# A planner with new step durations, a table of rank offsets, and a first layer that starts unit by unit

## The chip, the cores and the metric

The kernel runs on one core of a Trainium2 chip. The metric is the device time of one execution in microseconds (us), the median of several runs. TensorE (PE) does the matrix products, VectorE (DVE), ScalarE (ACT) and GpSimd (POOL) the elementwise work, and SyncE (SP) issues the transfers.

## The reference

Causal attention over 576 positions with 8 heads and 2 batches, mixed with a linear memory read-out, then two feed-forward layers in sequence:

```python
scores = scale * q @ k.T; scores[causal] = -1e9
local = softmax(scores) @ v
mem_out = (phi(q) @ M_prev) / (phi(q) @ z_prev + 1e-6)
x = g * mem_out + (1 - g) * local            # 1152 x 512
h = x @ w_in; x = elu(h) @ w_out             # 512 -> 2048 -> 512
p = probs / probs.sum(-1)
out = sum_e p[:, e] * (relu(x @ w1[e]) @ w2[e])   # 4 experts, 512 -> 1024 -> 512
```

## The kernel before

Each fp32 product is made of three products of rounded parts (`mm3`, L276: high x high, high x low, low x high). For each matrix the high part is an ACT copy to the rounded type, and the low part, here called the remainder, a subtraction on POOL (`part_l`, L247) or DVE. `w_in` and `w_out` come as 64-bit floats: each half tile of such a weight is loaded, then `upper` on ACT, `shift` and `lower` on DVE make an fp32 half of it (L211 to L238), which is also kept in DRAM for the second use.

The tokens are cut in two. Units F0 to F3 (two heads each) do attention for the first 384 tokens; units R00 to R13 for the other 768. A unit's steps (`plan_unit`, L1186) are named in the code: load, split_h/split_l (high part and remainder of queries and keys), phi (the memory features), mem, score, lowest, exp, trans, evac, values, sum, both, turn (a transposition), join (writes the input of the first layer). F3 is the "hurried" unit. While the R units run, the first 384 tokens go through the first layer (a0: four parts, each four "up" groups `ua` and four "down" groups `da`) and the experts (b0: `ub`, `db`). Then the R tokens go through both layers in a faster form with half sums (`Wide`; `plan_halves`; `x1.plan` makes the sums T1 to T4 of its input).

The order of instructions on each engine is written out by a planner (`Plan`, L1040). Every step has an engine, a cost in us, a rank, predecessors, and slots (buffers, PSUM banks) that it takes and gives. `order` runs a clock: an engine that is free takes the ready step with the lowest rank. For most slots the steps take them in the order in which they were added, whatever their rank; the banks "m" (three), "s0" and "s1" are exempt. The engines then run that order; semaphores make them wait for what they really need. A unit's rank is its start plus an offset per step (`OFFSET`, L163); R units start at 48 plus `STARTS2`, and none of their steps may start earlier than its rank less 4 (`EARLY`). A weight's rank is in `W_RANKS` (12, 26, 32, 38, 44) or follows the clock of the layer.

Where the plan sees PE wait over 0.3 us in the first 140 us, `keep_busy` puts products on a tile of zeros ahead of the step (L304), and at least one ahead of most PE steps of F units (`FEWEST`). `WARM` such products stand at the start.

A first-layer group takes one "m" bank and multiplies four chunks of 128 input rows (kk 0 to 3), which come from units F0 to F3 in this order. `group` (L344) puts it into the plan as two steps, kk 0 to 2 and kk 3; `before_up` (L358) makes both wait for all four units' joins. In F units the second score piece takes two "m" banks, a second transposition group and the turn one each.

## Time and profile before

| | us |
|---|---|
| median of 3 runs (718.53 to 719.46) | 719.34 |
| profiled execution | 718.8 |
| its span, first to last instruction | 717.0 |
| PE busy | 706.3 (99%) |
| POOL busy | 426.0 (59%) |
| DVE busy | 392.6 (55%) |
| ACT busy | 354.3 (49%) |

A PE that is shown as busy may run products on zeros; they have the line L304. "Releaser" names what ended a wait. In a table of windows each row is a stretch of the span: its length, the busy time of each engine with the number of its instructions, the granted TensorE clock, the share of the 16 DMA engines, and the rate.

### The profile page before, as it was taken

The page shows a single profiled execution, that of the slowest core. Times are in us where ns is not written, and L with a number is a line of the kernel's source. Part 1 is how long each engine was busy: PE and PEld are TensorE (multiplying, and loading weights), DVE is VectorE, ACT ScalarE, POOL GpSimd, SP SyncE. Part 2 cuts the span into 40 slices and gives each one's busy share as a digit, 9 for nine tenths or more (in the row PEclk, how much of TensorE's full clock was granted, in tenths as well). Part 3 has the DMA queues.
Part 4 walks back from the last instruction along what each step waited for, and adds up shares of the span by engine and source line. Part 5 has one row for each costly group of instructions (what it writes and reads, how often), then busy time and mean ns, then how long its engine had stood idle before and what let it go on. Part 6 is the DMA issues. An engine that isn't in the chain of part 4 may idle for free.

```text
span 717.0 us, 10716 instructions
## 1 busy us (share of the span) xinstructions
PE 706.3 (99%) x4099; PEld 640.0 (89%) x4099; DVE 392.6 (55%) x846; ACT 354.3 (49%) x610; POOL 426.0 (59%) x256
## 2 busy tenths in 40 slices
PE   9989999999999999998999999999999999999997
PEld 5769998988889889897999999998998989889896
DVE  3787785534453353454718466873645636354462
ACT  7868877453544443444867355752423423233120
POOL 5467886855546534179988564597646566564210
PEclk9999999999999999999999999999999999999999
DMA  8678983525133142031432111222211203121002
GB/s 288 231 266 319 370 324 118 195 95 172 53 127 118 49 129 88 31 118 59 133 118 89 59 59 59 62 80 66 88 60 59 92 26 118 35 83 59 1 1 88
DMA packets 23539, 82.21 MB, mean 115 GB/s; under 512 B 2880, under 2 KB 2880, under 8 KB 23488
## 3 DMA queue, kind: packets, MB, share of 16 engines
q1 hardware_dynamic: 23488, 81.53, 33.4%
q8 instruction: 32, 0.52, 0.3%
q14 instruction: 19, 0.16, 0.1%
HBM read 70.77 MB, written 10.75 MB: 114 GB/s over the span
## 4 chain that ended last, share of the span: by engine, by line
PE 88%; POOL 3%; DVE 3%; DMA 2%; ACT 2%; issue 1%; SPq 0%; DVEq 0%; ACTq 0%
PE db L278 9%; PE db L280 8%; PE db L279 8%; PE ov L1377 4%; PE da L278 4%; PE da L279 4%; PE da L280 4%; PE ub L278 3%; PE sR L1299 3%; PE tR L1361 3%; PE ub L280 3%; PE ub L279 3%; PE ov L1384 1%; PE om L1248 1%; PE ua L278 1%; PE ua L280 1%
## 5 line engine op out<-in xcount | busy, mean ns | idle before, releaser
L249 POOL TENSOR_TENSOR wl<-wr,wh 128x1024 fp32r<-128x1024 f32 x72 | 172.1, 2395 | 160.3 <-ACT wh L245 155.4
L245 ACT ACTIVATE wh<-wr 128x1024 fp32r<-128x1024 f32 x72 | 75.7, 1056 | 109.3 <-PE db L279 65.6
L278 PE MATMUL db<-wh,hb 128*128 128x512 f32 x288 | 115.0, 399 | 0.0
L280 PE MATMUL db<-wl,hb 128*128 128x512 f32 x288 | 112.7, 391 | 2.0 <-POOL wl L249 2.0
L279 PE MATMUL db<-wh,hb 128*128 128x512 f32 x288 | 112.3, 390 | 0.0
L997 DVE SCALAR_TENSOR_TENSOR acc<-db,pr,acc 128x512 f32<-128x512 f32 x42 | 31.5, 751 | 69.9 <-PE db L280 69.2
L280 PEld LDWEIGHTS db<-wl,hb 128*128 128x128 f32 x288 | 54.0, 188 | 13.9 <-POOL wl L249 2.4
L278 PE MATMUL da<-ha,wh 128*128 128x384 f32 x192 | 65.3, 340 | 0.0
L280 PE MATMUL da<-ha,wh 128*128 128x384 f32 x192 | 64.2, 335 | 0.0
L278 PEld LDWEIGHTS db<-wh,hb 128*128 128x128 f32 x288 | 54.2, 188 | 11.3 <-issue 1.4
L279 PE MATMUL da<-ha,wl 128*128 128x384 f32 x192 | 64.2, 334 | 0.0
L279 PEld LDWEIGHTS db<-wh,hb 128*128 128x128 f32 x288 | 54.2, 188 | 10.0
L278 PE MATMUL ub<-yh,wh 128*128 128x384 f32 x128 | 45.7, 357 | 0.0
L280 PE MATMUL ub<-yl,wh 128*128 128x384 f32 x128 | 43.0, 336 | 0.0
L279 PE MATMUL ub<-yh,wl 128*128 128x384 f32 x128 | 42.9, 335 | 0.0
L1377 PE MATMUL ov<-rvR,pfR 128*128 128x65 f32 x288 | 38.3, 265 | 0.0
L1377 PEld LDWEIGHTS ov<-rvR,pfR 128*128 128x128 f32 x288 | 37.2, 191 | 0.2
L278 PEld LDWEIGHTS da<-ha,wh 128*128 128x128 f32 x192 | 36.1, 188 | 0.5 <-issue 0.4
L279 PEld LDWEIGHTS da<-ha,wl 128*128 128x128 f32 x192 | 36.1, 188 | 0.0
L280 PEld LDWEIGHTS da<-ha,wh 128*128 128x128 f32 x192 | 36.0, 188 | 0.0
L1322 ACT ACTIVATE ptR<-ptR,nmR 128x576 f32<-128x576 f32 (+2 forms) x48 | 29.8, 659 | 10.3 <-DVE nmR L1313 10.2
L506 ACT ACTIVATE hb<-ub 128x384 fp32r<-128x384 f32 x32 | 15.7, 491 | 38.2 <-PE ub L280 38.2
(862 smaller groups left out, 1835.3 us busy)
## 6 DMA issues: line engine op xcount, KB each, us to landing
wr<-in_w SPq DMA_DIRECT2D x64, 512.0 KB, 3.7
w<-in_w SPq DMA_DIRECT2D x32, 512.0 KB, 6.5
wscr<-wr SPq DMA_DIRECT2D x16, 512.0 KB, 7.3
wr<-wscr SPq DMA_DIRECT2D x16, 512.0 KB, 3.3
rvR<-in_vm_r SPq DMA_DIRECT2D x8, 520.0 KB, 4.6
qkR<-in_qk_r SPq DMA_DIRECT2D x8, 480.0 KB, 4.9
rvF<-in_vm_f SPq DMA_DIRECT2D x4, 520.0 KB, 5.0
out<-acc SPq DMA_DIRECT2D x8, 256.0 KB, 2.0
```

Of the source, the lines that this page charges most:

```text
L245: nc.scalar.activation(out=t["wh"], in_=t["wr"], func=AF.Copy)
L249: nc.gpsimd.tensor_tensor(out=wl, in0=t["wr"], in1=f32(t["wh"]), op=ALU.subtract)
L278: nc.tensor.matmul(out, ah, bh, start=first, stop=False)
L279: nc.tensor.matmul(out, al, bh, start=False, stop=False)
L280: nc.tensor.matmul(out, ah, bl, start=False, stop=last)
L506: nc.scalar.activation(out=t["h"][:, 0], in_=t["ps"], func=AF.Relu)
L997: nc.vector.scalar_tensor_tensor(out=acc, in0=t["ps"], scalar=p, in1=acc, op0=ALU.mult, op1=ALU.add)
L1248: nc.tensor.matmul(pair("om", t, r0, r), unit["phi"][:, q:q + r], apart(MEMORY[kind] + 2 * bi), start=True, stop=True,)
L1299: nc.tensor.matmul(unit["s", odd, t, n][:, :w], unit[x][rows, q], unit[y][rows, ks[odd]], start=m == 0 and r0 == 0, stop=m == 2 and final,)
L1322: nc.scalar.activation(out=blk, in_=blk, func=AF.Exp, scale=-1.0, bias=unit["nm"][odd][:, k:k + 1])
L1361: nc.tensor.transpose(pst[:, P * n:P * n + P], src, ident)
L1377: nc.tensor.matmul(unit["ov"][:, odd, t], pf[:, col:col + P], unit["rv"][:, at_], start=False, stop=odd == 1 and j == nb - 1)
```

## The change

- The planner's cost functions and lags get other constants (`act_cost`, `dve_cost`, `values_cost`, `LAG`, some PE and DVE steps), and the least products on zeros are counted in PE steps.
- `Plan.alone`: steps in this set start only when POOL is free in the plan, and book POOL for their length. In it: `shift` and `lower` of the first three weights, the subtractions of the x sums, and `probs`.
- `MOVES`: offsets that `Plan.add` adds to the ranks, by unit, by step, by weight, by group.
- `before_up` of a0, part 0: kk 0 and 1 wait for F0 and F1, kk 2 for F2, kk 3 for F3; groups with fc over 1 wait for F3's turn besides. `group` takes a list of stages.
- F3's turn takes bank "t" in place of "m".
- F0's load is two transfers: keys first (`load_k`), then queries; its splits are three pieces, keys, the first 256 columns of queries, the rest. The first two scores wait for the first two pieces.
- `WARM` is 11 in place of 16; the plan's PE starts at `AWAKE`.

The diff, cut to its core:

```diff
+MOVES = {
+    ("F", "evac"): 6.5, ("F", "join_l"): -12, ("F", "load"): 3.5, ("F", "load_v"): -3, ("F", "phi_r"): 9,
+    ("F", "values"): -12, ("F0", "exp21"): 7, ("F0", "load_v"): 8, ("F0", "turn"): 14.5, ("F1", "exp21"): 13,
+    ("F1", "load"): 4, ("F2", "join_h"): 3.5, ("F2", "mem"): 5, ("F3", "score00"): 6.5, ("R", "exp"): -21.5,
+    ("R", "load_v"): -9, ("R", "mem"): -0.5, ("R", "phi_r"): -2.5, ("R", "score"): -17.5, ("R", "split_l"): 8.5,
+    ("R", "trans"): -10, ("R", "values"): -5.5, ("a0", "then", "d"): 8, ("a0", "then", "u", 1): -10.5,
...
+    ("v", "S2"): 14, ("v", 52): 4.5, ("w", "lower"): -11.5, ("w", "part_h"): 7, ("w", "part_l"): 16.5,
+    ("w", "shift"): 3.5, ("w", "upper"): -1.5, ("w", 0): 21, ("w", 1): 7.5, ("w", 14): 11.5, ("w", 2): -22.5,
+    ("w", 20): 18.5, ("w", 6): 14.5, ("w", 8): 4.5, ("w", 9): -20.5, "F0": 5, "F2": 9, "F3": 8, "R00": -28.5,
+    "R01": -28, "R02": -37.5, "R03": -9, "R10": -43.5, "R11": -6.5, "R12": -12.5,
+}
...
+        plan.alone.add(("probs",))
...
-    WARM = 16
+    WARM = 11
+    AWAKE = 2.66 + 0.218 * WARM
...
+                if i < W_EARLY:
+                    plan.alone |= {("w", i, f"{x}{half}") for x in ("shift", "lower")}
...
-            self.plan.add((*key, 0), "pe", 3 * cost, self.due, lambda: fn((0, 1, 2)), after, takes)
-            self.plan.add(key, "pe", cost, self.due, lambda: fn((3,)), [(*key, 0), *late], (), gives)
+            before, start = [], 0
+            for n, (upto, needs) in enumerate(stages):
+                name, last = (*key, f"k{n}"), upto == 4
+                self.plan.add(
+                    key if last else name, "pe", (upto - start) * cost + 0.04 * (n == 0), self.due,
+                    lambda kks=tuple(range(start, upto)): fn(kks), [*before, *needs], [] if n else takes, gives if last else (),
+                )
+                before, start = [name], upto
...
-            return [(f"F{c}", "join_l") for c in range(H // 2)], []
+            done = [[(f"F{c}", "join_l")] for c in range(H // 2)]
+            return [(2, done[0] + done[1] + [("F3", "turn")] * (fc > 1)), (3, done[2]), (4, done[3])]
...
+                    plan.alone.add((self.what, name, kk))
...
-        return 0.833e-3 * n + (0.09 if psum else 0.13)
+        return 0.833e-3 * n + (0.055 if psum else 0.095)
...
-        return 1.042e-3 * n + 0.115
+        return 1.042e-3 * n + 0.065
...
-        LAG = {"sync": 2.8, "pe": 0.2, "act": 0.13, "dve": 0.13, "pool": 0.1}
+        LAG = {"sync": 2.8, "pe": 0.2, "act": 0.16, "dve": 0.17, "pool": 0.12}
...
+            rank += sum(MOVES.get(x, 0.0) for x in families(key, engine))
...
+                        if key in self.alone:
+                            if free["pool"] > now + 1e-6:
+                                continue
+                            free["pool"] = now + cost
...
+        whole, keys, early = slice(0, nq + nk), slice(nq, nq + nk), slice(0, 2 * P)
+        if uid == "F0":
+            add("load_k", "sync", 0.8, lambda: load(keys), takes=["raw"])
+            add("load", "sync", 0.8, lambda: load(slice(0, nq)))
+            splits = [("0", keys, ["load_k"]), ("1", early, ["load"]), ("", slice(2 * P, nq), ["load"])]
...
-        x_from = "m" if spare else "t"
+        x_from = "m" if spare and not hurried else "t"
```

`families` gives the names under which a step looks up `MOVES`; all that match are added:

```python
def families(key, engine):
    name = str(key[0])
    if name[0] == "F":
        return [name, ("F", key[1].rstrip("0123456789")), key]
    if name[0] == "R":
        return [name, ("R", key[1].rstrip("0123456789"))]
    if name in ("w", "v"):
        return [(name, key[1]), (name, key[2].rstrip("0123456789") if name == "w" else key[2])]
...
```

## Rows read from the trace of the kernel before

**Rows 1.** Windows over the whole span: busy us of each engine, clock, DMA.
```profile
6.40:35.00 28.60, 28.07 (x248) 21.39 (x248) 19.03 (x83) 23.96 (x54) 15.75 (x11) 1.00 0.78 277
35.00:40.30 5.30, 4.31 (x29) 2.50 (x28) 4.45 (x9) 2.29 (x4) 1.70 (x1) 1.00 0.83 308
48.80:53.90 5.10, 3.50 (x22) 1.82 (x20) 4.82 (x10) 5.10 (x11) 5.10 (x5) 1.00 0.94 350
53.90:112.00 58.10, 57.81 (x366) 54.71 (x364) 48.49 (x97) 45.16 (x79) 44.13 (x28) 1.00 0.87 322
112.00:330.00 218.00, 218.00 (x1381) 194.01 (x1381) 98.76 (x252) 108.15 (x174) 122.26 (x69) 1.00 0.32 104
330.00:346.00 16.00, 13.58 (x66) 11.46 (x65) 5.03 (x9) 5.99 (x11) 15.53 (x10) 1.00 0.43 134
346.00:713.00 367.00, 367.00 (x1937) 343.99 (x1937) 203.81 (x377) 154.88 (x269) 213.57 (x120) 1.00 0.20 66
```

**Rows 2.** The same windows for the tile zeros alone (PE, PEld, DVE).
```profile
35.00:40.30 5.30, 2.56 (x12) 1.05 (x12) 0.00 (x0) 1.00 0.83 308
48.80:53.90 5.10, 2.38 (x12) 1.08 (x12) 0.00 (x0) 1.00 0.94 350
53.90:112.00 58.10, 1.27 (x7) 0.41 (x5) 0.00 (x0) 1.00 0.87 322
```

**Rows 3.** Waits of PE (total, times, longest), and the chain at 330 us.
```profile
PE db L280 <- POOL wl L249: 2.0, 1, 2.0
328.91 2.00 POOL xT4l L705 x2
330.91 2.31 POOL wl L249
```

**Rows 4.** Chain of waits from 35 to 59 us: start, us, what.
```profile
50.07 0.70 DVE wr L235
50.81 1.67 PE sR L304 x7
53.26 0.92 PE da L304 x5
54.18 0.17 PE da L278
```

**Rows 5.** Timeline: remainders of weights 0, 2 and 4, first uses of 0 and 4.
```profile
29.00 2.36 POOL L249 TENSOR_TENSOR wl<-wr,wh 128x1024 fp32r<-128x1024 f32 x1 [2.78 <-ACT wh L245]
40.27 0.47 PE L278 MATMUL ua<-xh,wh 128*128 128x384 f32 x1
44.68 2.42 POOL L249 TENSOR_TENSOR wl<-wr,wh 128x1024 fp32r<-128x1024 f32 x1 [3.71 <-ACT wh L245]
55.48 2.40 POOL L249 TENSOR_TENSOR wl<-wr,wh 128x1024 fp32r<-128x1024 f32 x1
58.35 0.44 PE L278 MATMUL ua<-xh,wh 128*128 128x384 f32 x1
```

**Rows 6.** The in-place shift (ns min/median/max), its longest, and POOL beside it.
```profile
L231 DVE TENSOR_SCALAR wr<-wr x6: 415/418/2180, 23.6 to 42.4; 128x512 int32<-128x512 int32 x6
38.60 2.36 POOL L249 TENSOR_TENSOR wl<-wr,wh 128x1024 fp32r<-128x1024 f32 x1 [5.72 <-ACT wh L245]
39.07 2.18 DVE L231 TENSOR_SCALAR wr<-wr 128x512 int32<-128x512 int32 x1
```

**Rows 7.** Timeline of the start, and the window with the highest DMA rate.
```profile
0.72 0.39 SPq L1164 DMA_DIRECT2D qkF<-in_qk_f  x1
4.06 0.99 ACT L1173 ACTIVATE qhF<-qkF 128x448 fp32r<-128x448 f32 x2 [2.07 <-DMA qkF<-in_qk_f]
6.41 0.36 PE L1299 MATMUL sF<-qhF 64*128 64x192 f32 x2
80.00:90.00 10.00, 10.00 (x60) 9.56 (x60) 8.39 (x17) 8.81 (x16) 8.75 (x6) 1.00 1.02 415
```

**Rows 8.** Chain of waits over the first 14 us.
```profile
2.10 6.55 DMA qkF<-in_qk_f
```

More of the change, by code (lines that the diff above doesn't have):

```diff
@@ L52 @@
 ]
+MOVES = {
[11 rows of a table added]
+}
[7 more added lines that the diff above has]
+        return [(name, key[1]), (name, key[2].rstrip("0123456789") if name == "w" else key[2])]
+    if name[0] in "ab":
+        return [(name, *key[1:3])] if engine == "pe" else [(name, "then", key[1]), (name, "then", key[1], key[-1])]
+    return [name, (name, key[1])] if name in "xy" else [name]
 def f32(ap):
@@ L342, in key, with group @@
             return (self.name, *a)
-        def group(self, key, cols, after, late, takes, gives, fn):
+        def group(self, key, cols, stages, takes, gives, fn):
             cost = 3 * (cols / 2400 + 0.0132)
@@ L382, in up @@
                 last = nb == len(self.blocks) - 1
-                early, late = self.before_up(part, fc)
+                first, *rest = self.before_up(part, fc)
                 self.group(
-                    key, n, [self.weights(part, fc // 2), *early], late,
+                    key, n, [(first[0], [self.weights(part, fc // 2), *first[1]]), *rest],
                     ["m"] + ["h"] * (nb == 0), ["w"] * (last and fc % 2), products,
@@ L544, in down @@
                 self.group(
-                    key, 512, [self.weights(part, 2), self.weights(part, 3), self.last_up(part)]
-                    + self.units(part, 0, 1, 2),
-                    self.units(part, 3), ["m"], (["w"] * 2 + ["h"] * 4) * last, products,
+                    key, 512,
+                    [(3, [self.weights(part, 2), self.weights(part, 3), self.last_up(part)] + self.units(part, 0, 1, 2)),
+                     (4, self.units(part, 3))], ["m"], (["w"] * 2 + ["h"] * 4) * last, products,
                 )
@@ L1047, in __init__ @@
             self.awake, self.last = 0.0, 0.0
+            self.alone = set()
         def add(self, key, engine, cost, rank, fn, after=(), takes=(), gives=(), slack=0.0, early=1e9):
+            rank += sum(MOVES.get(x, 0.0) for x in families(key, engine))
             self.steps[key] = (engine, cost, rank, fn, after, takes, list(gives), slack)
             self.first[key] = rank - early
-        def as_added(self):
-            for step in self.steps.values():
-                step[3]()
         def order(self, free=None):
@@ L1159, in add, with load @@
             )
-        def load():
-            unit["k"] = atile([P, NQ + KEYS["R"]], F32, tag="raw", name=f"qk{uid}")[:, :nq + nk]
-            nc.sync.dma_start(out=unit["k"], in_=qk[kind][c] if kind == "F" else qk[kind][b, c])
+        def load(cs):
+            if "k" not in unit:
+                unit["k"] = atile([P, NQ + KEYS["R"]], F32, tag="raw", name=f"qk{uid}")[:, :nq + nk]
+            nc.sync.dma_start(out=unit["k"][:, cs], in_=(qk[kind][c] if kind == "F" else qk[kind][b, c])[:, cs])
         def load_v():
@@ L1170, in split_h @@
         def split_h(cs):
-            if cs.start == 0:
+            if "h" not in unit:
                 unit["h"] = atile([P, NQ + KEYS["R"]], F32R, tag="qh", name=f"qh{uid}")[:, :nq + nk]
@@ L1175, in split_l @@
         def split_l(cs):
-            if cs.start == 0:
+            if "l" not in unit:
                 unit["l"] = atile([P, NQ + KEYS["R"]], F32R, tag="ql", name=f"ql{uid}")[:, :nq + nk]
@@ L1197, in phi @@
             nc.gpsimd.tensor_tensor(out=unit["phi"], in0=unit["e"], in1=unit["phi"], op=ALU.add)
-        add("load", "sync", 1.6, load, takes=["raw"])
+        whole, keys, early = slice(0, nq + nk), slice(nq, nq + nk), slice(0, 2 * P)
[3 more added lines that the diff above has]
+            splits = [("0", keys, ["load_k"]), ("1", early, ["load"]), ("", slice(2 * P, nq), ["load"])]
+        else:
+            add("load", "sync", 1.6, lambda: load(whole), takes=["raw"])
+            splits = [("", whole, ["load"])]
         add("load_v", "sync", 1.3, load_v, takes=["rv"])
-        pieces = [("0", slice(0, nq)), ("", slice(nq, nq + nk))] if uid == "F0" else [("", slice(0, nq + nk))]
-        for name, cs in pieces:
-            n, first = cs.stop - cs.start, cs.start == 0
-            add("split_h" + name, "act", act_cost(n), lambda cs=cs: split_h(cs), ["load"], ["qh"] * first)
+        for name, cs, loaded in splits:
+            n, first = cs.stop - cs.start, name == splits[0][0]
+            add("split_h" + name, "act", act_cost(n), lambda cs=cs: split_h(cs), loaded, ["qh"] * first)
             eng = ("dve", dve_cost(n)) if uid == "F0" else ("pool", pool_cost(n))
@@ L1210, in plan_unit @@
         if kind == "F":
-            add("phi_p", "act", act_cost(nq), phi_p, ["phi_e", "split_l"], gives=["raw"])
+            add("phi_p", "act", act_cost(nq), phi_p, ["phi_e", *(f"split_l{x}" for x, _, _ in splits)], gives=["raw"])
             add("phi", "pool", pool_cost(nq), phi, ["phi_p"], gives=["pe"])
@@ L1330, in plan_unit @@
                 f"score{t}{n}", "pe", score_cost(t, z_ - a), lambda t=t, n=n: score(t, n),
-                ["split_l"] + ["score{}{}".format(*pieces[0])] * (not first), s_from[t, n] + ["pt", "nm", "nm"] * first, ["qh", "ql"] * last,
+                [f"split_l{x}" for x, _, _ in splits[:2 if t < 2 else 3]] + ["score{}{}".format(*pieces[0])] * (not first), s_from[t, n] + ["pt", "nm", "nm"] * first, ["qh", "ql"] * last,
             )
@@ L1335, in plan_unit @@
                 add(
[L1336 removed]
+                    f"lowest{t}{n}{odd}", "dve", dve_cost(z_ - a) + 0.015,
                     lambda odd=odd, t=t, n=n: lowest(odd, t, n),
@@ L1441, in plan_unit @@
         add("turn", "pe", 0.11 * nt, turn, ["both"], [x_from], ["tv"])
-        done = [("m", (uid, "turn")) if spare else "t"]
+        done = [("m", (uid, "turn")) if x_from == "m" else "t"]
         if group:
@@ L1472, in tile_kernel @@
         plan, clock = Plan(SLOTS), [START2]
-        plan.awake, plan.last = IDLE_END, 0.43 * WARM - 0.5
+        plan.awake, plan.last = IDLE_END, AWAKE
         plan_small(plan, OFFSET["load"] + 3.0, 1.5)
@@ L1485, in tile_kernel @@
         x1.plan(plan, START2 + STARTS2[-1] + 8.0, lambda name, kk: [(f"R{b}{c}", "join_l") for b, c in units])
-        free = plan.order({"pe": 0.43 * WARM - 0.5})
+        free = plan.order({"pe": AWAKE})
     ps_g = ctx.enter_context(tc.tile_pool(name="ps_g", bufs=8, space=PSUM, reuse_waits="tile"))
```

32 lines of the change are left out of this document (16 added, 16 removed), and 2 rows, old and new, of the table MOVES.

## The prediction

> **What bounds the kernel now.** I read the stretches first. From 346 us to 713 us TensorE (PE) is busy all of the time, and so it is from 112 to 330 us; in these two stretches it runs real products back to back, so nothing that the planner reorders there can shorten them [rows 1]. That leaves 0 to 112 us and 330 to 346 us. A busy PE hides something there: the products on "zeros", which only keep the engine awake, count as work. The same windows for that tile alone show where [rows 2]. In 35.0 to 40.3 us PE is busy 4.31 us, 2.56 of it on zeros, so it works about 1.75 of 5.3 us and 3.6 us are lost. In 48.8 to 53.9 us it is 3.50 less 2.38, or 1.1 of 5.1 us, and 4.0 us are lost. In 53.9 to 112 us 1.3 us of zeros and 0.3 us of idle time are lost, 1.6 in all; in 330 to 346 us 2.4 us, of which 2.0 us is one wait for a weight remainder from GpSimd (POOL) [rows 3]. The zeros of 6.4 to 35 us I leave out: the kernel puts at least one ahead of most attention steps of the early units in either version. With 1.0 us at the start (below) the list is 1.0 + 3.6 + 4.0 + 1.6 + 2.4 = 12.6 us. That is what an order without any stall could win.
>
> **First layer unit by unit.** Before, every group of the first layer waits in the plan until all four early units F0 to F3 are joined. After, its first two input chunks wait for F0 and F1 only, the third for F2, the fourth for F3. The groups of fc 0 and 1 may open early, fc 2 and 3 only behind F3's turn. The opened groups can thus run three chunks of three products each ahead of F3's end: 2 x 9 = 18 products at 0.17 us [rows 4], or 3.1 us of real work into the 3.6 us that are lost now between 35.0 and 40.3 us. Weight 0, which both groups read, is ready at 29.00 + 2.36 = 31.4 us, 8.9 us ahead of its first use at 40.27 [rows 5], so there is room. The price is banks: an open group holds one of three "m" banks, and a second score piece of an F unit takes two of them at once. So the second group can only open once F3 has had that piece. F3's turn gets the bank "t" instead of "m", so that it can't wait for the groups that wait for it. Bounds: 0 (groups open only when F3 is done) and 3.1 us; I take 2.3, nearer to the upper, because most of the lost time lies behind F3's scores.
>
> **Ranks, durations, and the stall at 49 to 54 us.** The durations and ranks run nowhere; they change the order alone. The last row ahead of the stall is the conversion of a weight in the score banks: DVE's wr step at 50.07 us ends, then PE goes on with seven zeros, R00's scores, five zeros and the first down group [rows 4]. PE had nothing else: the R units may not start before their rank less 4, and R00's rank was 48. Now R00's ranks fall by 28.5 and its scores' by 17.5 more, R10's by 43.5, R02's by 37.5. So R00's scores can stand ahead of weights 3 and 4 in the score banks, and PE has R products to run while a weight is made. The down group reads weight 2, made by 44.68 + 2.42 = 47.1 us [rows 5], ahead of 48.8 us, where PE runs dry. So both things that PE lacked can be there. Bounds: 0 and 4.0 us; I take 2.5.
> What takes it back: weight 4 is ready at 55.48 + 2.40 = 57.88 us and used at 58.35 [rows 5], with 0.5 us to spare. Whatever PE gains before has to be gained by weight 4 too, or filled with R products. DMA is the tight resource there, 0.87 busy over 53.9 to 112 us and 0.94 from 48.8 [rows 1]; in 0 to 53.9 it has room. A weight's loads keep their order in either version (their slots go in the order in which the steps were added, whatever the rank), so weight 2's rank of 9.5 can't bring it ahead of weights 0 and 1. I subtract 0.5 us, between 0 and the whole 2.5.
>
> **Steps that need GpSimd idle.** An in-place shift of a weight half takes 0.42 us at the median of six and 2.18 us once: it began at 39.07 while a GpSimd subtraction of 2.36 us ran from 38.60, and it ended just after that one [rows 6]. So 1.8 us of DVE are lost, and the join of F3, next but one on DVE, with the first-layer product that reads it, stood behind it. In the new plan the shift, the "lower" step, the subtractions of the x sums and the "probs" step start only when GpSimd is free, and book it for their length. DVE does something else meanwhile. What it costs: GpSimd is kept off, at 0.4 to 0.7 us a step, 21 steps in all. That is hidden where POOL has room (55% at 6.4 to 35 us), not at 330 to 346 us, where it is busy 15.53 of 16 us [rows 1]. Two-sided: +0.3 (a row of that size in the first layer) to -1.0; I take +0.2, counted with the 1.6 us of 53.9 to 112, of which I take 0.5 in all.
> The Trainium skill's page "SBUF — State Buffer" (section "SBUF: two separate sides") states that whichever of DVE and GpSimd starts first holds the shared pair for the whole instruction and the other fully blocks. The row agrees with it. By that rule the wait is not removed but handed to GpSimd, which speaks against this part; it is the third rival.
>
> **330 to 346 us.** PE waits 2.0 us for a remainder that POOL makes at 330.91, behind those of the x sums, T4's last [rows 3]. These can't begin before the last unit R13 is joined. R13's scores come 17.5 earlier in rank, its exps 21.5, its values 5.5, so its join should come some us sooner; but the remainder's own rank falls back by 16.5. Bounds -1 and +2.4; I take +1.2.
>
> **Start.** F0's 416 KB (448 columns of queries, 384 of keys) are issued at 0.72 us and the first split starts at 4.06, so 3.3 us. At 415 GB/s, the rate of 80 to 90 us, the bytes take 1.0 us, the rest 2.3. The keys alone (192 KB) then land at 0.72 + 2.3 + 0.5 = 3.5 us; the queries are the third issue, at some 1.6 us (0.4 us each), and land at 1.6 + 2.3 + 0.55 = 4.45. The pieces that the first score needs are then 256 columns of queries instead of the whole: behind two more splits of 0.3 us, DVE's remainder is done near 5.1 us. Warm-up ends five products earlier, 5 x 0.24 = 1.2 us [rows 4, 7]. So the first score moves from 6.41 to about 5.4 us, by 1.0 us. Fewer warm-up products could cost clock; the granted clock reads 1.00 in each stretch [rows 1], so I book nothing.
> Against this, the ranks put F1's values (520 KB) ahead of F1's queries and keys in SP's queue. That transfer, issued at 2.10 us, is the longest link of the chain of waits here with 6.55 us, to 8.65 us [rows 8]. 520 KB more ahead of it are 1.25 us at 415 GB/s, 1.9 at 277 GB/s [rows 1, 7]. Together -0.9 to +1.0; I take 0.3.
>
> **Sum.** 2.3 + 2.5 - 0.5 + 0.5 + 1.2 + 0.3 = 6.3 us. The profiled execution took 718.8 us around a span of 717.0; the median of the runs is 719.34, 0.5 us above it. 719.34 - 6.3 = 713.0 us.
>
> **Rivals.**
> The first is the forecast: stalls filled, 709 to 716 us, chance 0.58.
> Second, the weights take it back: PE reaches weight 4 earlier, which has 0.5 us to spare, and waits there; weights 8 and 12 follow behind a DMA that is 0.87 busy. Then of the gain before 54 us only 0.5 us is left, and 1.2 at 330 us and 0.5 between: 2.2 us, or 717.1 us. For it: the half microsecond and the DMA share. Against: R products now stand ready, and DMA has a quarter to spare in the first 50 us. Chance 0.15.
> Third, the waits only change hands: GpSimd, kept off by 21 steps, is late with remainders by what DVE gains, and the order as a whole moves stalls instead of closing them (also the case that the table does nothing on the chip). 718 to 720.5 us, about 719.3. Chance 0.10.
> Fourth, slower: weight 0 comes last. Its rank falls from 12 to 33, its high part's to 40 and its remainder's to 49.5, behind every step of F0 to F3. If DVE and ACT do it only after F3's last sums at 39 us, it still needs two "lower" halves (0.7 each), 1.06 us on ACT and 2.4 on POOL, and the first layer starts at about 44 to 45 us, not at 40.3, with the early opening lost: +4, less 1.5 from the rest, or 721.8 us. It decides from the point where weight 0 is ready after 40.3 us; ready after 35 us it already eats the early opening. For it: the ranks. Against: rank is only a priority, and ACT is idle 4.6 of the 28.6 us to 35 us [rows 1]. Chance 0.17.
>
> **How the numbers follow.** The likeliest is 713.0 us. All stalls gone gives 719.3 - 12.6 = 706.7, with 0.05 below it; the fourth rival reaches 721.8, and I stop at 721.5, with about 0.08 beyond. About 0.2% (1.4 us, under 717.9 and over 720.8) is what a measurement here can tell from no change. Faster: the first rival and nearly all of the second, 0.73. Same: most of the third with a rest of the second, 0.11. Slower: the fourth, less what of it stays small, and an end of the third, 0.16.
>
> **What would show it.** Right: real products on "ua" before F3's turn, zeros between 35 and 54 us well under 5 us, first score near 5.4 us, no shift over 0.7 us, no wait of 2 us near 330. Wrong: the first "ua" after 40 us with a weight remainder just ahead of it; a wait for weight 4 of more than 2 us; PE gaps behind 112 us that are not there now.

## The result, and the profile after

The changed kernel takes 710.72 us (median of four runs, 708.95 to 713.1) where the kernel before, run beside it, takes 719.40 us: a ratio of 0.988, 95% interval 0.985 to 0.992. That is 8.7 us, 2.4 us more than the 6.3 us forecast, and inside the range. One thing is needed to read every number below: the runs of this kernel fall into two groups, 707 to 709 us with a mean granted TensorE clock of 1.00, and 712 to 713 us with 0.993 to 0.994. The profiled execution is of the second group: 713.1 us around a span of 711.2 us. So the profile shows a gain of 5.8 us of span and, inside it, a loss that the kernel before didn't have.

The same windows as in [rows 1], over the profile after (length, busy us of PE, PEld, DVE, ACT, POOL with instructions, granted clock, DMA share, GB/s):

```profile
27.30:28.80 1.50, 0.07 (x2) 0.05 (x1) 0.55 (x2) 1.50 (x4) 1.37 (x2) 1.00 0.96 366
28.80:39.50 10.70, 10.70 (x59) 8.05 (x60) 7.68 (x29) 6.22 (x13) 8.32 (x6) 0.54 0.59 211
48.80:53.90 5.10, 5.10 (x39) 5.03 (x38) 4.38 (x10) 4.36 (x10) 3.34 (x3) 1.00 0.68 243
53.90:112.00 58.10, 57.98 (x379) 54.08 (x378) 44.53 (x93) 46.42 (x83) 42.26 (x28) 1.00 0.83 290
112.00:330.00 218.00, 217.54 (x1346) 194.78 (x1345) 100.99 (x246) 106.23 (x169) 128.21 (x71) 1.00 0.34 113
330.00:346.00 16.00, 16.00 (x88) 15.14 (x87) 8.90 (x17) 9.72 (x16) 15.92 (x9) 1.00 0.53 168
```

And the tile zeros alone, as in [rows 2] (PE, PEld, DVE):

```profile
35.00:41.00 6.00, 1.95 (x4) 0.41 (x4) 0.00 (x0) 0.59 0.39 119
41.00:50.00 9.00, 0.25 (x1) 0.00 (x0) 0.00 (x0) 1.00 0.89 287
50.00:705.00 655.00, 0.00 (x0) 0.00 (x0) 0.00 (x0) 1.00 0.31 104
```

Read the two together. From 48.8 to 346 us PE is busy but for 0.6 us, and none of it is zeros; before, 4.0 us were lost in 48.8 to 53.9 us and 1.6 us behind that. The stall at 330 us is gone too: 16.00 of 16 us. But in 28.8 to 39.5 us the granted clock is 0.54, nearly all of it at the lower of its two levels (0.50, which is 1.2 GHz). As an estimate from this row, at the full level up to 10.7 x (1 - 0.54) = 4.9 us of that stretch would not have been needed. PE had stood still just ahead of it, in 27.3 to 28.8 us. The waits of PE (in all, times, longest) name the wait:

```profile
PE ov L1437 <- ACT pfF L1421: 1.4, 1, 1.4
PE db L312 <- DVE hb L552: 0.5, 1, 0.5
```

The 2.0 us wait for a weight remainder of [rows 3] isn't in the list any more; the second line is the only later wait, and it is new (0.46 us between 112 and 330 us). The first comes from ACT's order. The chain of waits (first row) and the timeline (start, us, engine, line, what, idle time before it) tell how:

```profile
19.06 6.68 DMA qkR<-in_qk_r
25.82 1.00 ACT L1220 ACTIVATE qhR<-qkR 128x960 fp32r<-128x960 f32 x1 [1.99 <-DMA qkR<-in_qk_r]
28.12 0.58 ACT L1421 ACTIVATE pfF<-tF 128x512 f32<-128x512 f32 x1
28.75 0.49 PE L1437 MATMUL ov<-rvF,pfF 128*128 128x130 f32 x2 [1.43 <-ACT pfF L1421]
```

R00's queries and keys now come early. Their transfer takes 6.68 us, and ACT, which runs its list in order, stands 1.99 us in front of their split. Behind the split stand a phi step, a weight half, F1's join and then the evacuation of F2's transposed probabilities (`pfF`), for which PE waits. R00's split is in no hurry at all; F2's evacuation is.

The early opening of the first layer, on PE (the products between the first and the last row of a run of `ua` are left out, as is other work):

```profile
43.64 0.55 PE L1475 MATMUL xF<-ident,tvF 128*128 128x128 f32 x3
43.94 0.42 PE L311 MATMUL ua<-xh,wh 128*128 128x384 f32 x1
...
45.96 0.34 PE L313 MATMUL ua<-xl,wh 128*128 128x384 f32 x1
...
47.63 0.49 PE L1475 MATMUL xF<-ident,tvF 128*128 128x128 f32 x3
47.88 0.42 PE L311 MATMUL ua<-xh,wh 128*128 128x384 f32 x1
```

Between F2's turn (first row) and F3's turn (the row ahead of the last) stand 12 products of the first layer; behind F3's turn come 12 more, which run while F3's join is made.

### The profile page after: what moved, and what is told of

Same layout as the page of the kernel before. It is cut to its first block, busy times and chain, and to the rows that moved or that the text cites. A ratio compares the mean times of both kernels' runs of the same rounds, so it can differ in the third digit from the quotient of the medians.

```text
span 711.2 us, 10664 instructions
## 1 busy us (share of the span) xinstructions
PE 703.9 (99%) x4063; PEld 639.8 (90%) x4063; DVE 389.5 (55%) x847; ACT 353.5 (50%) x611; POOL 426.9 (60%) x256
## 4 chain that ended last, share of the span: by engine, by line
PE 93%; DMA 2%; ACT 2%; DVE 1%; POOL 0%; issue 0%; SPq 0%; ACTq 0%; POOLq 0%
PE db L311 9%; PE db L312 9%; PE db L313 9%; PE da L311 4%; PE da L313 4%; PE da L312 4%; PE ov L1430 4%; PE ub L311 3%; PE ub L313 3%; PE sR L1352 3%; PE ub L312 3%; PE tR L1414 3%; PE ua L311 2%; PE ua L312 2%; PE ua L313 1%; PE ov L1437 1%
## 5 line engine op out<-in xcount | busy, mean ns | idle before, releaser
L311 PEld LDWEIGHTS db<-wh,hb 128*128 128x128 f32 x288 | 54.1, 188 | 11.4 <-issue 0.7
L313 PEld LDWEIGHTS db<-wl,hb 128*128 128x128 f32 x288 | 54.1, 188 | 11.4
L312 PEld LDWEIGHTS db<-wh,hb 128*128 128x128 f32 x288 | 54.1, 188 | 11.3 <-DVE hb L552 0.9
L552 DVE SCALAR_TENSOR_TENSOR hb<-ub,hb 128x384 fp32r<-128x384 f32 x32 | 17.8, 557 | 29.6 <-ACT hb L549 29.1
```

Of the source, the lines that this page charges most:

```text
L311: nc.tensor.matmul(out, ah, bh, start=first, stop=False)
L312: nc.tensor.matmul(out, al, bh, start=False, stop=False)
L313: nc.tensor.matmul(out, ah, bl, start=False, stop=last)
L552: nc.vector.scalar_tensor_tensor(out=t["h"][:, 1], in0=t["ps"], scalar=0.0, in1=f32(t["h"][:, 0]), op0=ALU.max, op1=ALU.subtract)
```

## The experiments

The theory that this profile suggests: at a held clock every stall of the list (35 to 40 us, 49 to 54, 54 to 112, 330 to 346) is closed, which is worth about 11 us; the profiled execution gave 5 to 6 us of that back because PE stood still behind R00's late transfer and its clock fell. The rivals: the loss is part of the new order and always there; or single parts of the change carry the gain and the rest is along for the ride.

The first three experiments ask about the clock. The next five leave out a part, or put one part alone into the kernel before, and let the planner plan anew. The last four change one thing and keep the order of every engine.

**The changed kernel once more, unaltered.**

> The changed kernel, unaltered, beside the next three. Theory (clock): its executions fall into two groups, some 709 us with a granted clock of 1.000 and some 713 us with 0.993, and the difference lies in 28.8 to 39.6 us, where the profiled execution had a granted clock of 0.5 behind a PE wait of 1.8 us. Rival (spread): times lie anywhere between 708 and 714 us and the clock of the records doesn't go with them.

Measured: 707.59 us median (707.38, 707.21 and 707.8 with the clock at 1.00, 712.28 at 0.993); ratio 0.986 [0.983, 0.989]. The profile is of an execution at full clock, with a span of 705.6 us, 11.4 us under that of before. Its windows, and ACT's split of R00:

```profile
27.30:28.80 1.50, 1.50 (x16) 1.32 (x15) 1.17 (x6) 1.50 (x4) 1.50 (x2) 1.00 0.86 230
28.80:39.50 10.70, 10.47 (x88) 8.04 (x85) 9.73 (x35) 8.24 (x17) 9.15 (x7) 1.00 0.83 299
24.07 1.01 ACT L1220 ACTIVATE qhR<-qkR 128x960 fp32r<-128x960 f32 x1 [0.79 <-DMA qkR<-in_qk_r]
```

ACT waits 0.79 us for R00's transfer here and not 1.99, the evacuation comes in time, and the clock holds. Of the 5.6 us between the two profiles of one and the same kernel, 0.45 us are there from the start (PE's steps from 6.7 to 26 us begin that much later), 1.3 us come with the wait at 28 us (1.43 us by its row, not the 1.8 of the expectation), and 3.9 us build up behind it, to 40 us, at the lower clock. So the loss isn't part of the order as such; between these two executions it hangs on when a transfer lands.

This profile also gives the gain stage by stage, as lost time of PE (length less busy, plus zeros), in [rows 1, 2] and here. 35.0 to 40.3 us: 3.55 before, 0.39 after. 48.8 to 53.9: 3.98 and 0. 53.9 to 112: 1.56 and 0.10. 112 to 330: 0 and 0.47. 330 to 346: 2.42 and 0. That is 10.6 us; the first score comes at 5.63 us where it came at 6.41 [rows 7], another 0.8. Together 11.4 us, the difference of the spans. That it meets so exactly is luck: 6.4 to 35 us and 40.3 to 48.8 us, which this list leaves out, lose 1.0 us less as well, and PE's products other than zeros take 1.0 us more in all (685.2 us against 684.1).

**Zeros in front of the wait.** Seven more products on zeros ahead of F2's first values, where PE stood still:

```diff
-            keep_busy(at[what], FEWEST[kind])
+            keep_busy(at[what], FEWEST[kind] + 7 * ((uid, what) == ("F2", "ov")))
```

> The changed kernel with seven more products on zeros ahead of F2's first values, where PE stood still from 27.3 to 28.75 us. Theory (the fall of the clock follows from that stand-still): the granted clock stays at 1.00 in 27 to 40 us, every execution takes 708 to 710 us, none 712 to 713. Rival (the clock falls for another reason, as the warm-up that is five products shorter): both groups stay, median 709 to 713 as before. Third: the products themselves delay the values, +0.5 us and no more.

Measured: 709.16 us (707.91 to 709.42 at full clock, 712.89 at 0.995, the profiled one). So the theory's "none 712 to 713" is missed. The zeros cover the old place, and in the profiled execution the clock falls at another, some 9 us later. PE's wait, the two steps behind which it stands, and windows around it:

```profile
PE sR L1352 <- DVE nmR L1366: 1.6, 1, 1.6
33.12 2.54 POOL L280 TENSOR_TENSOR wl<-wr,wh 128x1024 fp32r<-128x1024 f32 x1
33.48 2.74 DVE L266 SCALAR_TENSOR_TENSOR wr<-w,wr 128x512 int32<-128x512 int32 x1
34.00:36.00 2.00, 1.11 (x9) 0.78 (x7) 2.00 (x1) 1.46 (x4) 1.97 (x2) 1.00 0.25 102
36.00:38.00 2.00, 1.28 (x8) 0.84 (x9) 1.97 (x9) 0.00 (x0) 1.24 (x1) 0.96 0.31 74
38.00:40.00 2.00, 2.00 (x11) 2.00 (x10) 1.97 (x7) 1.34 (x2) 0.00 (x0) 0.50 0.91 250
```

So it isn't the place that matters but a stand-still like it, wherever it falls. Its cause is another than at 28 us: ACT doesn't wait for R00's transfer here. DVE's `lower` step (L266), which is in the set that needs GpSimd idle, takes 2.74 us beside a remainder that GpSimd began 0.36 us earlier, and ends 0.56 us behind it; the other five of its kind take 0.69 us. The row minimum of R00's scores (`lowest`), for which PE waits, stands behind it on DVE. In the unaltered kernel at full clock the same step began at 32.41 us, ahead of that remainder (33.20 us) and 0.38 us behind a shorter GpSimd step (`ppR`, 1.21 us), and took 1.39 us. So some 1 us of shift in time decides beside which step it falls, although the plan keeps them apart. Covering one place of PE doesn't cure what ACT or DVE hands on to the next.

**R00's split later.** The split is planned 2.5 us behind its transfer's reckoned end, so that ACT does F2's evacuation, F1's join and a weight half first. Of the other steps only neighbours change places: on ACT the evacuation and a weight half also pass F1's join, on DVE its own part of the evacuation passes one step, and two transfers swap in SP's queue; in the traces PE's and GpSimd's orders are the same:

```diff
-  takes, gives, slack.get(engine, 0.0),
+  takes, gives, 2.5 if (uid, key) == ("R00", "split_h") else slack.get(engine, 0.0),
```

> The changed kernel with one step moved: R00's split on ACT is planned 2.5 us after its transfer's planned landing, and so stands behind F2's first evacuation, F1's join and one weight half in ACT's order; nearly all else keeps its order. Theory (the stand-still at 27 us comes from this split, which waits on ACT for R00's transfer while the evacuation that PE needs stands behind it; the clock falls after it): PE's wait for the evacuation stays under 0.6 us in the profile, the granted clock 1.00 in 27 to 40 us, and no execution takes over 710 us; 706.5 to 708.5. Rival (the late transfer hurts anyway, through R00's scores): the two groups stay, with the wait at R00's scores near 35 us. Rival (the clock falls by chance): one execution in three at 711 to 713 us.

Measured: 707.88 us (707.08 to 708.88), ratio 0.985 [0.983, 0.986], the clock at 1.00 in all four runs. In its profile ACT doesn't wait for R00's transfer, and F2's evacuation is done ahead of the split:

```profile
24.94 0.59 ACT L1421 ACTIVATE pfF<-tF 128x512 f32<-128x512 f32 x1
27.25 1.00 ACT L1220 ACTIVATE qhR<-qkR 128x960 fp32r<-128x960 f32 x1
```

The cause of the lower clock in the first profiled execution is thereby named, and it is gone in this version. That three of the eight executions of the changed kernel fell and none of these four is in line with it; alone it would be a small count, and four more of the same order with five more zeros at the start (the last experiment) held their clock too. The other two executions of the changed kernel at the lower clock have no profile, so that theirs had the same cause isn't shown. This version is 11.3 us under the kernel before run beside it (719.23) and steady; of the versions that held their clock in every run it is the fastest.

**The first layer waits for all four units, planned anew.**

```diff
-            return [(2, done[0] + done[1] + [("F3", "turn")] * (fc > 1)), (3, done[2]), (4, done[3])]
+            return [(3, sum(done, [])), (4, [])]
```

> The changed kernel with the first layer's part 0 waiting for all four early units again (chunks 0 to 2 at once), everything else as changed. Theory (the staging is worth 2 us): 2 to 3 us slower than the changed kernel, with PE on zeros or idle ahead of F3's turn. Rival (R00's products fill that time, the staging is worth nothing): within 1 us of the changed kernel. As the ranks were chosen with the staging, up to 2 us more can come from an order that no longer fits.

Measured: 716.80 us, ratio 0.997 [0.995, 0.999]; the runs at full clock 714.1 to 715.4, those at 0.992 to 0.995 718.2 to 720.3. Against 707.2 to 707.8 of the changed kernel at full clock, leaving this part out of the plan costs some 7 us, more than the 2 to 3 expected. The profile (full clock) shows the hole behind F3's turn:

```profile
42.07 0.49 PE L1475 MATMUL xF<-ident,tvF 128*128 128x128 f32 x3
44.11 1.67 PE L337 MATMUL tR<-zeros 128*128 128x512 bf16 x7 [1.54 <-DVE xl L1483]
45.61 0.60 PE L1414 MATMUL tR<-ident,ptR 128*128 128x128 f32 x4
```

From F3's turn to the next product that isn't zeros pass 3 us: R's transposition and the first layer both wait for F3's join (`xl`). The stall at 330 us stays closed in this version (PE 16.00 of 16 us there), so that one belongs to another part.

**Steps that need GpSimd idle: the set is ignored, planned anew.**

```diff
-                        if key in self.alone:
+                        if False:
```

> The changed kernel without the steps that need GpSimd idle: the set is ignored. Theory (these steps matter little): within 1 us of the changed kernel, with one or two shifts of 1 to 2 us among the first six. Rival (they are a main part): 3 us slower or more. By the rule of the Trainium skill's page SBUF - State Buffer (the pair is held for the whole instruction) the blocked time should show again in DVE's shifts, where GpSimd runs beside them.

Measured: 720.27 us, ratio 1.002 [1.001, 1.003]: the whole gain is gone. The in-place shift (ns min/median/max) stands beside GpSimd work again, and PE waits for two joins that DVE makes (`xl`):

```profile
L262 DVE TENSOR_SCALAR wr<-wr x6: 427/759/1496, 12.8 to 34.2; 128x512 int32<-128x512 int32 x6
PE tR L337 <- DVE xl L1483: 1.7, 1, 1.7
PE tF L337 <- DVE xl L1483: 1.5, 1, 1.5
```

Six shifts take 5.1 us here and 2.5 us in the version with the later split (median 0.42). The Trainium skill's page "SBUF — State Buffer" (section "SBUF: two separate sides") states that, for certain kinds of DVE instruction, whichever of the two engines comes first holds the shared pair and the other blocks; the median of 0.76 us, where GpSimd is not kept off, agrees. The six `lower` steps take 6.9 us against 4.8, one of them 2.73 us; the join for which PE waits 1.5 us stands behind that one on DVE. But 4.7 us of DVE are not 12 us of the kernel. Part of the rest is the clock, 0.50 in 27 to 30 us of this profile, behind that wait; for what is left I have only the argument that the plan, without this set, is another plan.

**The empty table.** `MOVES = {}`, all else as changed, planned anew.

> The changed kernel with an empty table: new durations, staging, GpSimd-idle steps and split transfer stay, all ranks are those of before. Theory (the table is the main part, as it sets where R00 stands): 717 to 722 us, with PE idle again near 50 us. Rival (the structure does it, staging above all): 711 to 714 us.

Measured: 720.13 us, ratio 1.002 [1.001, 1.004], with two of the ten executions at 724.5 and 724.9 us (clock 0.988 and 0.986). Without the table the stall at 330 us is back, and there are waits among the F units; the one near 50 us comes back in part only (1.6 us lost in 48.8 to 53.9 us, where it was 4.0):

```profile
PE pa10S L300 <- POOL swl48S L653: 2.8, 1, 2.8
PE tF L1402 <- ACT ptF L1363: 2.6, 4, 1.0
```

**The kernel before with the R units' entries of the table alone.** `MOVES` with the keys that begin with R, and the line of `Plan.add` that applies them, put into the kernel before.

> The kernel before with the table's entries for the R units alone, and nothing else of the change. Theory (R00's earlier rank closes the stall at 49 to 54 us by itself): 2.5 to 4 us faster than before, zeros gone from 48.8 to 53.9 us. Rival (R00 ahead of F3 costs F3 as much, since the first layer still waits for all four units): within 1.4 us of before, zeros or waits moved to 35 to 45 us. A wait over 1.5 us in 25 to 40 us could also lower the clock there, by some 4 us.

Measured: 719.71 us, ratio 1.000 [0.998, 1.001]; 716.9 to 717.4 us in the four runs at full clock, 719.7 to 720.4 in the six at 0.994. The profile (full clock) says what R's ranks do:

```profile
48.80:53.90 5.10, 4.19 (x25) 3.34 (x26) 4.18 (x10) 3.96 (x8) 4.58 (x4) 1.00 0.78 202
330.00:346.00 16.00, 16.00 (x83) 14.55 (x82) 6.60 (x12) 7.05 (x12) 12.85 (x7) 1.00 0.46 149
48.72 1.11 PE L1397 MATMUL ov<-rvR,pfR 128*128 128x65 f32 x8 [1.24 <-DVE pfR L1386]
314.24 0.45 PE L298 MATMUL ub<-yh,wl 128*128 128x384 f32 x1 [1.22 <-POOL wl L268]
```

At 330 us they close the stall of 2.4 us, but a wait of 1.22 us for a weight remainder is new at 314 us (last row), which takes half of that back. At 48.8 to 53.9 us there are no zeros now, 4.19 us of products where there were 1.1; but what is won is lost again elsewhere: from 40.3 to 48.8 and from 53.9 to 330 us, 7.8 us are idle or zeros here where it was 1.8 us. In the end the runs at full clock are 2.1 us faster. The stall at 49 to 54 us is closed whole in the changed kernel and in the version that waits for all four units; without the set, the table or the split transfer 1.6 to 3.6 us are lost there.

**The first transfer in one, planned anew.** One load of F0, three splits kept, the first 256 columns of queries now ahead of the keys.

> The changed kernel with F0's queries and keys in one transfer again; the three splits stay. Theory (the split brings 0.3 us and no more): first score within 0.5 us of that of the changed kernel, which came at 6.3 and 5.6 us. As the order is planned anew from the first step, the whole can still lose several us where the table no longer fits: 708 to 717 us. Rival (the split is worth 1 us, as worked out at first): first score at 6.4 us or later.

Measured: 720.63 us, ratio 1.002 [1.000, 1.003], the clock at 0.993 to 0.997 in every run, and over the 717 us expected at most. The first score comes at 5.81 us, as the theory has it. The largest wait:

```profile
PE sR L1352 <- DVE nmR L1366: 2.4, 1, 2.4
```

Four parts left out one at a time (the stages, the set, the table, the split transfer) bring 9, 13, 13 and 13 us over the 707.6 us of the whole change, which itself gains 8.7 to 11.5 us. These are no prices of parts. A new plan is another order throughout, and the table was searched for one plan. So the last four experiments all start from the version with R00's split later (707.88 us), leave the plan as it is and change only what is issued.

**First-layer products together, in the same order.** The products of the groups fc 0 to 3 of part 0 are all issued at the place of the last stage:

```diff
+            if key[:3] != ("a0", "u", 0):
+                return lambda: fn(kks)
+            return (lambda: fn((0, 1, 2, 3))) if last else (lambda: None)
```

> The kernel after with R00's split held back, as in the run that was 707.9 us, in the same order on every engine; only the products of the first four groups of the first layer (fc 0 to 3) are all issued at the place of the last stage, where the fourth input chunk comes in. This is the unit-by-unit start taken away without a new plan. Theory (the 12 products ahead of F3's turn, 38.9 to 41.1 us in that run, are real work moved into time that would be lost): PE waits there for up to 2.1 us, 708.5 to 710.0 us; with the granted clock falling behind that stand-still, as it did behind the one at 27 us, up to 714. Rival (R00's scores, issued next, come earlier and cover it, so that the gain of the unit-by-unit start lay in the other order that it lets the plan have): 707.4 to 708.4 us.

Measured: 712.62 us (711.35 to 714.08; the fastest at a clock of 1.00, the others at 0.996 to 0.997), ratio 0.990 [0.989, 0.992]. At full clock that is 3.4 us over the version it was made from (profile against profile), more than the 2.1 us that I gave as the most. The profile has the hole of the version that waits for all four units, in the same place:

```profile
41.37 0.49 PE L1480 MATMUL xF<-ident,tvF 128*128 128x128 f32 x3
43.64 0.66 PE L1419 MATMUL tR<-ident,ptR 128*128 128x128 f32 x4 [1.78 <-DVE xl L1488]
39.00:45.00 6.00, 3.69 (x24) 2.99 (x25) 5.48 (x16) 5.36 (x10) 5.97 (x3) 1.00 0.89 321
```

PE works 3.69 of 6 us in the window where it works 6.00 of 6 in the version with the products stage by stage. Ahead of F3's turn 0.8 us are lost, from 38.2 to 41.4 us: R00's scores, issued next, come earlier there and cover most of the first dozen's place, as the rival has it. Behind the turn it is 1.78 us, where the second dozen hides F3's join. The rival's time, 708.4 us at most, is passed by 3 us, so the staged products are worth time in this order; most of it is the second dozen's.

**F0 in the first transfer, in the same order.** All 832 columns in the first, the second issues nothing.

```diff
-            add("load_k", "sync", 0.8, lambda: load(keys), takes=["raw"])
-            add("load", "sync", 0.8, lambda: load(slice(0, nq)))
+            add("load_k", "sync", 0.8, lambda: load(whole), takes=["raw"])
+            add("load", "sync", 0.8, lambda: None)
```

> The same kernel of 707.9 us with F0's 832 columns all in the first of its two transfers; the second issues nothing, the three splits and the order stay. This is the first transfer in one without a new plan. Theory (splitting it is worth little, since the query half landed last in either case): 707.2 to 708.6 us. Rival (the keys' early split is what brings the first score forward): the first score 0.5 to 1 us later, 708.4 to 709.2 us.

Measured: 707.81, 708.17, 709.14 and 709.31 us at full clock, 716.25 at 0.990 (the profiled one). The first score, at 5.57 us in its profile, isn't later than with the split (5.63 us at best), so the rival's reason falls. At full clock the split transfer is worth 0 to 1 us, the size given. The execution at the lower clock shows the same mechanism as R00's, at another transfer: ACT in order in front of F1's late queries and keys, PE without F0's exponentials, and then the lower clock:

```profile
10.59 0.90 ACT L1220 ACTIVATE qhF<-qkF 128x832 fp32r<-128x832 f32 x1 [2.16 <-DMA qkF<-in_qk_f]
13.16 0.33 PE L1414 MATMUL tF<-ident,ptF 128*128 128x128 f32 x1 [2.22 <-ACT ptF L1375]
13.20:28.00 14.80, 14.80 (x81) 11.00 (x82) 9.46 (x33) 11.28 (x24) 7.90 (x6) 0.55 0.76 257
```

**No least zeros, in the same order.** The products on zeros that stand ahead of most steps of F units in any case are left out (`0 * FEWEST[kind]` in the three places where they are issued); those for a wait that the plan sees stay.

> The same kernel of 707.9 us, in the same order, without the products on zeros that stand ahead of most attention steps of F0 to F3 whether the plan sees a wait or not (some 27 of 0.35 us between 6.3 and 35 us; those that the plan puts in for a wait stay). Theory (up to 35 us other engines set the pace, and the zeros only keep PE awake): at a held clock 706.5 to 708; with it, more short stand-stills, after which the granted clock falls, 710 to 714 us. Rival (PE itself sets the pace up to 35 us, and the zeros, 9.4 us of it, are paid for in time): 700 to 705 us.

Measured: 706.05, 706.32 and 707.0 us at 0.997 to 1.00, and 714.37 at 0.988 (the profiled one). 9.4 us of zeros stand between 6.3 and 35 us in the profile of the version that this one is made from; leaving most of them out wins 0.9 to 1.8 us. So up to 35 us PE doesn't set the pace; the zeros fill time that is lost anyway. What they are paid for may be seen in the fourth execution, one of a small count. Two stand-stills (a wait of 0.9 us and short ones around it near 19 us, one of 2.6 us near 37, the latter behind a `lower` step of 2.73 us beside a remainder on GpSimd), each with the lower clock behind it:

```profile
20.00:28.00 8.00, 8.00 (x44) 7.15 (x43) 4.66 (x16) 5.97 (x15) 4.10 (x3) 0.50 0.73 242
36.30:39.00 2.70, 0.64 (x5) 0.44 (x6) 2.67 (x8) 0.73 (x2) 2.59 (x2) 1.00 0.06 9
39.00:47.00 8.00, 8.00 (x39) 6.79 (x38) 5.30 (x16) 5.05 (x7) 4.04 (x2) 0.57 0.84 237
```

**Sixteen products at the start, in the same order.** `range(WARM + 5)` where the start's products on zeros are issued.

> The kernel of 707.9 us in the same order, with 16 products on zeros at the start in place of 11; the planner still reckons with 11. Theory (the 11, with the two zeros behind them, end about when the first score's input comes, so that five more at 0.22 to 0.43 us push the first score back by 1 to 2 us, and the start passes that on): first score at 7.3 to 8.5 us, 708.6 to 710 us. Rival (ACT sets the pace behind the first scores, so a later first score is taken up before 35 us): first score as late, 707.2 to 708.4 us. A third case, in which the longer start keeps the granted clock up where it falls otherwise, can't be told here, since it held in each run of the kernel of 707.9 us.

Measured: 709.17 us (708.9 to 709.31), 1.3 us over 707.88. The first score comes at 7.80 us; in the version with eleven it comes at 6.52:

```profile
0.97 6.46 PE L337 MATMUL warm<-zeros 128*128 128x512 bf16 x16 [0.97 <-DVE zeros L136]
7.80 0.36 PE L1352 MATMUL sF<-qhF 64*128 64x192 f32 x2
```

The first score comes 1.28 us later and the end 1.1 us later by the spans (707.3 and 706.2). Little of what is lost at the start is caught up, though PE isn't the bound up to 35 us; I take it that the chain of ACT, DVE and PE that is the bound there starts with that score.

## Why the prediction was right, and where it wasn't

The direction, the likeliest case and the range held. The sum held less well than its result: at full clock the gain is 11.4 us of span, nearly all of the 12.6 us that the prediction gave as the ceiling, and not 6.3; a loss that I booked at nothing then takes back some 5 us in some executions. The median of the four runs lies between two such executions of each kind. That the profiled one, 713.1 us, meets 713.0 is two errors that cancel.

**First layer unit by unit (2.3 us of 3.6).** Right mechanism, too small. I counted 18 products ahead of F3's end. There are 24: twelve ahead of F3's turn, twelve more behind it while F3's join is made. The six more fit the first two chunks of a third group, which may open behind F3's turn; I had counted only the two groups that may open ahead of it. 24 products at 0.17 us are 4.1 us of work, and the stretch's loss fell by 3.2 us. Taking the stages away in the same order costs 3.4 us at full clock, most of it behind F3's turn.

**Ranks and the stall at 49 to 54 us (2.5 less 0.5).** R products stand ready and the stall is closed whole, 4.0 us. PE waits for no weight behind it, so the half microsecond at weight 4 took nothing back, and the second rival falls. The step that failed is the reason: I gave R00's ranks the credit. They alone fill that window to 0.9 us, but open other waits for more than that; the gain there needs the rest of the order.

**Steps that need GpSimd idle (0.2, within 0.5).** At full clock the third rival, that the wait is only handed on, falls by the time: 53.9 to 112 us lost 0.10 us instead of 1.56, POOL's 16 busy us at 330 us held nobody up, and no shift is over 0.7 us in the profile of the changed kernel at full clock. But what the planner keeps apart isn't always apart on the chip. I looked at the shift alone; the `lower` step of the same set takes 1.39 us once even at full clock, twice its 0.69, beside a GpSimd step of R00 (`ppR`), and the remainder that GpSimd begins meanwhile takes 2.82 us and not 2.4. In the first profile, where PE and with it all else runs late, one shift takes 2.11 us beside a GpSimd subtraction, against the sign given ("no shift over 0.7 us"); with zeros in front of the wait and without the least zeros a `lower` of 2.73 to 2.74 us stands ahead of the stand-still behind which the clock fell. In those executions the wait is handed on to PE. Which part of the 0.5 us forecast for 53.9 to 112 us is this set's isn't shown.

```profile
34.83 2.35 POOL L280 TENSOR_TENSOR wl<-wr,wh 128x1024 fp32r<-128x1024 f32 x1
35.36 2.11 DVE L262 TENSOR_SCALAR wr<-wr 128x512 int32<-128x512 int32 x1
```

**330 to 346 us (1.2, between -1 and 2.4).** The whole 2.4 us came, less a new wait of 0.46 us between 112 and 330 us, one of the signs given for being wrong. R's ranks alone close the stall, as the kernel before with R's entries shows, but there a new wait of 1.22 us at 314 us takes half of it back. The mechanism named, the R units' earlier joins, is right: the last of their joins (DVE's `xB22l`) starts at 302.4 us in the changed kernel at full clock and at 302.1 us with R's entries alone, where it was 318.4 us before and 315.0 us with the empty table.

**Start (0.3, between -0.9 and +1.0).** The first score was to come at 5.4 us. It comes at 5.63 us at best and at 6.26 us in the first profile, so 0.8 and 0.15 us are won of the 1.0. Two terms were off against each other. The queries: I let them land at 4.45 us; ACT starts their split at 5.61 us in the profiled execution and at 5.16 us in the one at full clock. The price of F1's values ahead of F1's queries and keys: I took 1.25 to 1.9 us; ACT's split of F1 starts at 9.14 us at full clock and 9.59 us in the profiled execution, against 8.66 before, so 0.5 to 0.9. The five products of the start were right: 1.2 us reckoned, 1.1 to 1.3 measured. Splitting the transfer itself is worth 0 to 1 us.

**Clock (nothing).** This is the step that failed outright. I read 1.00 in each stretch of the kernel before and concluded that the clock was no matter; as a rival I thought of the shorter warm-up alone. In the kernel before PE was given zeros wherever the plan saw a wait; that this kept the clock up is in line with the version without the least zeros, but isn't shown. The new order has waits that the plan does not see, behind a transfer that lands late or a DVE step that meets GpSimd's, and PE then stands still without zeros; in the first profile the lower clock behind one of them costs 3.9 us.

**Fourth rival.** Weight 0 isn't last. The remainder just ahead of the first `ua` at 43.94 us ends at 34.83 + 2.35 = 37.2 us, with 6.8 us to spare, rank 49.5 or not (36.0 for a first `ua` at 38.36 us at full clock). The bound of 35 us, from which I saw the early opening eaten, was too strict: F2's turn, behind which the opening stands on PE, comes later still.

Not settled: which of the stand-stills lower the clock; what the executions at the lower clock that have no profile have in common; why the executions at full clock differ by up to 1.9 us (707.2 to 709.1); and what each part is worth by itself, which has no answer where each part changes the plan of all others. An order-keeping trial of the GpSimd-idle set wasn't made: the set is nothing but the order.

## What to carry to other kernels

Where an order is planned ahead, take from the profile the lost time of each stretch with filler work subtracted: here the sum of it, 12.6 us, was nearer to the 11.4 us that this searched order gives at full clock than the cautious shares taken from it (6.3). An engine that runs in order must not have a step that waits for a long transfer ahead of a step that the bounding engine needs soon: plan such a step by the latest landing, not by the mean (with 2.5 us of slack the four runs lie at 707.1 to 708.9 us, where the eight without it lie at 707.2 to 713.1). Two steps that must not run beside each other need a margin in time as well: an order on each engine alone doesn't keep them apart. And when a part of a planned order is to be priced, hold the order and change what is issued; leaving the part out of the plan prices the plan.

## What the runs showed of the hardware

The granted clock falls behind some short stand-stills of PE and not behind others. It fell to 0.50 or near behind waits of 1.43 us (the changed kernel, 28 us), 1.61 us (zeros in front of the wait, 36 us), 2.22 us (F0 in one transfer, 12 us) and 2.59 us (no least zeros, 37 us), and stayed low for some 7 to 14 us. It held at 1.00 behind 1.78 us (products together, 43 us), 1.68 us (F0 in one transfer, 43 us) and 1.72 us (the set ignored, 51 us), and in the kernel before with its 1.6 us wait near 50 us, between zeros. So the length of the wait alone doesn't tell.

The row of the granted clock reads 1.00 over the first 6.3 us of each profile, but the products of the start don't run at it: eleven of 512 columns start at 0.97 us and the next product at 5.64 us, 0.42 us each, where seven from 44.11 to 45.61 us in the version that waits for all four units, also at a clock of 1.00, take 0.21 us each. In the second profile of the unaltered kernel the pitch falls to 0.22 us within the eleven; its first score comes 0.63 us earlier, and the queries' split 0.45. The Trainium skill's page "TensorE: Matmul & The Clock Gate" (section "Wait — 56ns, not 53.3ns?") gives 426.7 ns for 512 columns at 1.2 GHz, which agrees with the pitch and not with the row.

DVE's `lower` step takes 0.69 us as a rule. Where it began 0.36 to 0.38 us behind a GpSimd step, it ended 0.54 to 0.56 us behind that one's end each time: it took 1.38 to 1.39 us beside a step of 1.2 us (the changed kernel at full clock, R00's split later), and 2.73 to 2.74 us beside a subtraction of 2.5 us (zeros in front of the wait, F0 in one transfer, no least zeros).

One and the same transfer differs between executions of one kernel by 1.3 us: R00's, issued at 19.06 us, held ACT until 25.82 us in one profile; issued at 18.61 us, until 24.07 us in the other, 6.8 and 5.5 us. What lengthened it isn't known.
